# Half-block loads in 2 KB rows, turned by a permuted identity, with a new order for the opening

## The chip, the core and the metric

The kernel runs on one core of a Trainium2 chip. A core has a matrix engine (PE, with its weight loads, PEld, listed apart), a vector engine (DVE), a scalar engine (ACT), a general engine (POOL) and a queue engine (SP) that issues most DMAs. The metric is the device time of one execution in microseconds. The kernel before takes 397.38 us, the median of three runs (397.12 to 397.79).

## The reference

```python
def _attn_ref(x, f_logit, lower_bound):          # (4, 6144, 256), (4, 6144, 256), (256,)
    sig = 1.0 / (1.0 + np.exp(-f_logit))
    f = lower_bound[None, None, :] + (1.0 - lower_bound[None, None, :]) * sig
    i = 1.0 - f
    for t in range(S):
        h = f[:, t] * h + i[:, t] * x[:, t]
        y[:, t] = h

def _moe_ref(x, w1, w2, w_out):                  # x: (24576, 256), the y of above
    g = np.maximum(x @ w1, x @ w2)               # (24576, 1024)
    return g @ w_out                             # (24576, 256), float32
```

A gated recurrence runs over 6144 tokens of each of four sequences, 256 channels wide; a maxout layer with 1024 hidden units and an output projection follow, token by token.

## The kernel before

The 24576 tokens are cut into 48 blocks of 512. The recurrence wants channels on partitions and tokens along the row (scan, L142, runs along the row), while the inputs have tokens first, so every block must be turned.

The maxout is rewritten as max(h1, h2) = h1 + relu(h2 - h1). The hidden matmuls use wd, the scaled difference of w2 and w1; the h1 part goes straight to the output by a 256 x 256 matrix w13, the product of w1 and w_out. A block so has 16 hidden matmuls of 512 columns (L245), eight relus (L240) and 40 output matmuls of 256 columns (L268).

Blocks 4 to 47 come in pairs: a DMA from POOL casts them to bf16 in DRAM (cast, L167), a DMA transpose from SP brings them in turned (turn_dma, L176), and the loop at L565 goes over blocks and hidden units, PE's hidden matmuls of block j beside the output of block j - 1. That part is the same in both kernels.

Blocks 0 to 3 are the opening, and the change lies there. They are loaded as they lie, in f32, by SP (load, L96): blocks 0 to 2 in halves of 256 tokens (256 KB), block 3 whole. Partition p gets token q * 128 + p for row q of a tile, so a packet is one token's 1 KB. ACT forms u = sigmoid(-f) (gate_nat, L107), DVE v = u * x (drive_nat, L112), both bf16. PE turns each (turn_pe, L120) by four transposes of 128 x 128 against the bf16 identity ident_b into a bf16 PSUM tile; forget (L132) makes the decay from the turned u on ACT or DVE, and the scan takes the decay and the turned v.

At the same time the weights come in as twelve loads of 256 KB, four quarters k of each of w1, w2 and w_out, and are prepared: rounded (RW, RO), subtracted (D), scaled (SC), w1 turned (TW), copied out of PSUM (KW), multiplied into w13 (W13) and kept (KL).

The order of all this is written out by hand in two lists. LOADS (L445) is the order on SP. f0a is the first half of block 0's f, x0b the second half of its x, w13 the quarter 3 of w1. At most eight of SP's loads are in flight: the ninth waits for the landing of the first that holds its semaphore. PLAN (L449) is the order of the compute steps; each engine runs its own steps in this order and waits where an input is late. In a step's name G is gate, V drive, TU and TV the turns of u and v, F forget, S scan, H a hidden matmul group, R relu, P and L output matmuls, O the copy of an output tile; digits are block, half (a, b) and channel half or unit; the ending .a, .v or .p names ACT, DVE or POOL. warm3 is three matmuls on zeros that keep PE busy. CA starts the first cast and the first DMA transposes.

[...]

Of the kernel before, what the change touches and what calls it, by code (L numbers as in the profile page):

```python
# [8 lines left out]
FP32 = mybir.dt.float32  # L9
BF16 = mybir.dt.bfloat16  # L10
ALU = mybir.AluOpType
AF = mybir.ActivationFunctionType
P = 128
# [3 lines left out]
def kernel(  # L17
# [13 lines left out]
    nc = tc.nc  # L31
# [4 lines left out]
    KC = D // P  # L36
    FC = DFF // P
    TB = 512
    HB = TB // 2
    NQ = TB // P  # L40
# [8 lines left out]
    const = ctx.enter_context(tc.tile_pool(name="const", bufs=1))  # L49
# [14 lines left out]
    ps_d = ctx.enter_context(tc.tile_pool(name="ps_d", bufs=5, space=PS))  # L64
    ps_o = ctx.enter_context(tc.tile_pool(name="ps_o", bufs=3, space=PS))

    ident = const.tile([P, P], FP32)
    ident_b = const.tile([P, P], BF16)
    warm = const.tile([P, TB], BF16)
    held = const.tile([P, 1], FP32)  # L70
    om = const.tile([P, KC], FP32)
# [10 lines left out]
    w13 = wpool.tile([P, KC, D], BF16)  # L82


    ins, us, vs, uT, vT, ffs, ys = {}, {}, {}, {}, {}, {}, {}

    def alloc_in(j):
        fn = inpool.tile([P, NQ, D], FP32, name="fn")
        xn = inpool.tile([P, NQ, D], FP32, name="xn")
        ins[j] = (fn, xn)  # L90
        us[j] = natpool.tile([P, NQ, D], BF16, name="un")
        vs[j] = natpool.tile([P, NQ, D], BF16, name="vn")
        ffs[j] = nffpool.tile([P, KC, TB], BF16, name="nff")
        ys[j] = ypool.tile([P, KC, TB], BF16, name="y")

    def load(j, s, half=None):  # L96

        src = (f_logit, x)[s]
        q0, q1 = (0, NQ) if half is None else (2 * half, 2 * half + 2)
        nc.sync.dma_start(  # L100
            out=ins[j][s][:, q0:q1, :],
            in_=src[0, j * TB + q0 * P : j * TB + q1 * P, :].rearrange(
                "(q p) d -> p q d", p=P
            ),
        )

    def gate_nat(j, q0, q1):  # L107
        nc.scalar.activation(  # L108
# [10 lines left out]

    def turn_pe(j, s, x):  # L120

        dst = (uT, vT)[s][j, x] = ps_d.tile([P, KC, HB], BF16, name="dT")
        src = (us, vs)[s][j]
        for q in range(2):
            for h in range(KC):
                nc.tensor.transpose(  # L126
                    dst[:, h, q * P : (q + 1) * P],
                    src[:, 2 * x + q, h * P : (h + 1) * P],
                    ident_b[:],
                )  # L130

    def forget(o, i, h, on_act=False):  # L132
# [43 lines left out]
    def turn_dma(c):  # L176
        for s, name in enumerate(("fs", "xs")):
            t = ttpool.tile([P, KC, CB * TB], BF16, name=("fT", "xT")[s])
            turned[c, s] = t
            nc.sync.dma_start_transpose(out=t[:], in_=spare[c % NS, name][:])  # L180

    def cast_behind(c):

        if c + 1 < NCH:
            last = CB * TB - 1
            nc.gpsimd.tensor_copy(out=held[:], in_=turned[c, 0][:, KC - 1, last : last + 1])  # L186
            cast(c + 1)
# [5 lines left out]
    def gate(j):  # L193
        ffs[j] = midpool.tile([P, KC, TB], BF16, name="ff")
        ys[j] = ypool.tile([P, KC, TB], BF16, name="y")
        us[j] = midpool.tile([P, KC, TB], BF16, name="u")
        nc.scalar.activation(out=us[j][:], in_=part(j, 0), func=AF.Sigmoid, scale=-1.0)  # L197

    def drive(j):
        vs[j] = midpool.tile([P, KC, TB], BF16, name="v")  # L200
        nc.vector.tensor_tensor(out=vs[j][:], in0=us[j][:], in1=part(j, 1), op=ALU.mult)  # L201

    def forget_half(j, h, on_act=False):
        forget(ffs[j][:, h, :], us[j][:, h, :], h, on_act)

    def scan_half(j, h):
        scan(j, h, 0, TB, vs[j][:, h, :])
# [45 lines left out]
    def hidden(j, fc):  # L253
        hidden_whole(j, fc)
        relu(j, fc)
# [49 lines left out]
    def project(j, slot):  # L305
        i, half_ = divmod(slot, 2)
        n = FC + KC
        project_steps(j, i, half_ * n // 2, (half_ + 1) * n // 2)
# [17 lines left out]
    def store(j, g):  # L326
        copy_out(j, g)
        send_out(j, g)

    def store_row(j, g, r):  # L330
        osb = lastpool.tile([P, D], FP32, name="row")
        nc.vector.tensor_copy(out=osb[:], in_=pos[j, g, r][:, 0, :])  # L332
        r0 = j * TB + 2 * g * P
        nc.sync.dma_start(
            out=out[r0 : r0 + 2 * P, :].rearrange("(p r) d -> p r d", r=2)[:, r, :],
            in_=osb[:],
        )
# [93 lines left out]
    def keep_warm(n):  # L431
        for _ in range(n):
            nc.tensor.matmul(  # L433
                idle[:].rearrange("p r d -> p (r d)"),
                lhsT=warm[:, 0:P],
                rhs=warm[:],
                start=True,
                stop=True,
            )
# [3 lines left out]


    LOADS = """  # L445
    f0a x0a f0b w13 w23 x0b w12 w22 wo3 w10 w20 w11 wo2 w21 f1a x1a wo0 f1b x1b wo1
    f2a f2b x2a x2b f3 x3
    """
    PLAN = """  # L449
    G0a RW3.p keeps_T keeps V0a TU0a D31.p warm3 TV0a D30.p G0b F0a0.v warm4 TU0b  # L450
    D21.p F0a1.v S0a1 S0a0 V0b F0b1.a warm1 TW3 F0b0.a RW0.p warm5 TV0b RW2.v S0b1
    D01.p KW3.a TW2 SC31.a SC30.a KW2.a S0b0 RO3.a H06a H07a D20.v SC21.a warm3 H06b
    SC20.v H07b D00.v W133 RW1.v R07.a TW0 H04b H04a RO2.p H05a R06.a P071 SC00.v
    H05b P070 P061 D10.p TW1 SC01.a KW0.v R05.a R04.v H01a KW1.v H00a H00b H01b P040
    P050 P060 G1a P041 SC10.v V1a W132 R01.a D11.p TU1a RO0.p SC11.a P051 TV1a R00.a
    H02a F1a1.v F1a0.a RO1.p H03b S1a1 P011 G1b H02b S1a0 P010 H03a R02.a W130 V1b
    P001 R03.a TU1b H17a F1b1.v P000 TV1b H15a F1b0.a S1b1 S1b0 G2a H16a P031 P030
    P021 G2b W131 KL1.v TU2a F2a0.a P020 H17b H15b KL0.v H16b L01 L11 R17.a TU2b
    H10a H10b R16.a V2a R15.v F2a1.v H11b O01.a P161 H11a TV2a F2b0.a H12b P151 L10
    P171 V2b H12a R11.a F2b1.v R10.a S2a1 TV2b S2a0 G3b P150 R12.a S2b1 G3a L00 S2b0  # L460
    H13a V3b TU3b O00.a H13b P101 R13.a F3b1.v H14a P160 F3b0.v H14b P100 P170 H20
    H26 V3a TU3a P111 F3a1.v H21 R14.a H27 R20.a F3a0.v R26.a TV3a S3a1 P120 H24
    TV3b R21.a P121 P110 S3a0 H22 R27.a S3b1 P130 R24.a R22.a S3b0 H23 P131 R23.a
    H25 P140 O10.v P141 R25.a O11.v CA
    """

    engines = {"a": nc.scalar, "v": nc.vector, "p": nc.gpsimd}
# [1 line left out]
    def load_item(name):  # L469
        if name[:2] == "wo":  # L470
            wout_load(int(name[2]))
        elif name[0] == "w":
            w, src = ((w1n, moe_w1), (w2n, moe_w2))[int(name[1]) - 1]
            weight_load(int(name[2]), w, src)
        else:
            half = ("ab".index(name[2]),) if len(name) == 3 else ()
            load(int(name[1]), "fx".index(name[0]), *half)
# [8 lines left out]
    def issue(item):  # L486
# [10 lines left out]
        elif kind in ("G", "V") and len(arg) == 2:  # L497
            (gate_nat if kind == "G" else drive_nat)(arg[0], 2 * arg[1], 2 * arg[1] + 2)
        elif kind in ("TU", "TV"):
            turn_pe(arg[0], "UV".index(kind[1]), arg[1])  # L500
        elif kind == "F" and len(arg) == 3:
            j, x, h = arg
# [48 lines left out]
    with tc.manual_schedule():  # L551
        for j in range(NP):
            alloc_in(j)
        nc.scalar.dma_start(out=lbr[:], in_=lower_bound.rearrange("(h p) -> h p", p=P))
        for name in LOADS.split():
            load_item(name)
        nc.vector.memset(warm[:], 0.0)  # L557
        make_identity(nc, ident[:])
        nc.vector.tensor_copy(out=ident_b[:], in_=ident[:])
        keep_warm(7)  # L560
        for item in PLAN.split():
            issue(item)
        assert not outs

        for j in range(3, NBLK + 1):  # L565
            for fc in range(FC):
                if j < NBLK:
                    hidden(j, fc)
                project(j - 1, fc)
                if fc == 0 and j > 3:  # L570
                    store(j - 2, 1)
                if fc == 4 and j < NBLK:
                    store(j - 1, 0)
                if j == NBLK and fc in (3, 5, 7):
                    if fc == 3:
                        store(j - 1, 0)
                    else:
                        store_row(j - 1, 1, (fc - 5) // 2)
                if (j, fc) in gate_of:
                    b = gate_of[j, fc]  # L580
                    gate(b)
                    drive(b)
                    for h in range(KC):
                        forget_half(b, h)
                        scan_half(b, h)
                if (j, fc) in turn_of:
                    turn_dma(turn_of[j, fc])
                    cast_behind(turn_of[j, fc])
# [30 lines left out]
```

## Time and profile before

| what | value |
|---|---|
| median of three runs | 397.38 us |
| the profiled execution | 397.38 us |
| its span | 395.6 us |
| PE busy | 387.6 us (98%) |
| ACT busy | 273.3 us (69%) |
| DVE busy | 251.2 us (63%) |
| POOL busy | 39.2 us (10%) |
| granted PE clock | full in all slices but the last (0.97) |
| first half-block load of f issued, landed | 0.74, 3.6 us |
| second half of block 0's x issued, landed | 3.29, 8.71 us |
| first hidden matmul of the loop over blocks | 36.0 us |

The page gives for each engine the time it was busy, as a share of the span. Busy time of PE is the union of pipelined matmuls, so a matmul's own duration (219 ns for 128 columns, 272 for 256) is longer than the step from one to the next; the steps are read from the chain of work that ended last, which follows back from the last instruction what released each one. The list of waits says for which producer an engine sat idle. The DMA view counts packets and the time they took as a share of sixteen DMA engines.

### The profile page before, as it was taken

Reading aid. Unit: us, or ns where it says so; the run is one execution under the profiler, and the core shown is the slowest. Engines: PE = TensorE matmul, PEld = TensorE weight load, DVE = VectorE, ACT = ScalarE, POOL = GpSimd, SP = SyncE. Lnnn points to the kernel's source line nnn. Section 1 sums busy time; section 2 is a strip of 40 time slices with the busy share of each in tenths; the row PEclk is TensorE's granted clock in tenths of the full one; section 3 lists DMA queues with packets and bytes.
Section 4 is the critical chain, followed back from the end, with each engine's and each line's share of the span. In section 5 each row is a group of like instructions: output and inputs, shape, how many; then the busy total and the mean of one; then the engine's idle time right before and its main releaser. Section 6 shows DMA issues by size and latency. Waiting matters only on the chain.

```text
span 395.6 us, 7146 instructions
## 1 busy us (share of the span) xinstructions
PE 387.6 (98%) x2793; PEld 275.0 (70%) x2840; DVE 251.2 (63%) x366; ACT 273.3 (69%) x451; POOL 39.2 (10%) x83
## 2 busy tenths in 40 slices
PE   8999999999999999999999999999999999999996
PEld 3796777676667777767677777666677777676775
DVE  4896965756755775576567656755775576567622
ACT  4787676677667666766676677667766766676661
POOL 2511011011101101001011011011011010100000
PEclk9999999999999999999999999999999999999999
DMA  7989999999999999999999999999898898981122
GB/s 252 350 220 211 211 206 216 216 221 225 200 228 201 203 230 178 229 220 202 199 232 209 188 228 191 195 208 230 198 204 213 186 202 193 217 188 55 53 81 107
DMA packets 125078, 79.12 MB, mean 200 GB/s; under 512 B 94194, under 2 KB 101620, under 8 KB 125044
## 3 DMA queue, kind: packets, MB, share of 16 engines
q1 hardware_dynamic: 113072, 55.59, 59.8%
q0 software_dynamic: 11968, 23.07, 35.7%
q8 instruction: 22, 0.36, 0.4%
q14 instruction: 12, 0.10, 0.1%
q10 hardware_dynamic: 4, 0.00, 0.0%
HBM read 53.48 MB, written 48.23 MB: 257 GB/s over the span
## 4 chain that ended last, share of the span: by engine, by line
PE 95%; DMA 1%; DVE 1%; issue 1%; SPq 1%; DVEq 0%
PE psO L268 53%; PE dT L245 39%; PE dT L225 2%; DMA xn<-in_x_dram 1%; PE dT L126 1%; SPq L100 0%; PE psO L413 0%; DVE vn L113 0%; SPq L344 0%; DVE y L149 0%; DVE wd L388 0%; DVE wdf L380 0%; DVE row L332 0%; PE dT L396 0%; DVEq L113 0%
## 5 line engine op out<-in xcount | busy, mean ns | idle before, releaser
L240 ACT ACTIVATE rt<-dT 128x512 bf16<-128x512 f32 x382 | 222.9, 596 | 104.4 <-PE dT L245 101.2
L268 PE MATMUL psO<-wob,rt 128*128 128x256 bf16 x1536 | 231.0, 273 | 0.2
L268 PEld LDWEIGHTS <-rt 128*128 128x128 bf16 x1536 | 150.0, 98 | 94.7 <-issue 0.2
L245 PE MATMUL dT<-y,wd 128*128 128x512 bf16 x690 | 208.8, 379 | 2.2
L149 DVE TENSOR_TENSOR_SCAN y<-ff,y,v 128x512 bf16<-128x512 bf16 x82 | 105.2, 1283 | 2.9
L317 DVE COPY osb<-psO 128x512 f32<-128x512 f32 x93 | 62.6, 678 | 65.6 <-PE psO L268 65.6
L245 PEld LDWEIGHTS <-wd 128*128 128x128 bf16 x736 | 72.0, 98 | 8.8
L268 PE MATMUL psO<-w,y 128*128 128x256 bf16 x384 | 72.4, 273 | 0.0
L201 DVE TENSOR_TENSOR v<-u,xT 128x1024 bf16<-128x1024 bf16 x44 | 30.4, 691 | 62.7 <-ACT u L197 50.8
L197 ACT ACTIVATE u<-fT 128x1024 bf16<-128x1024 bf16 x44 | 46.1, 1049 | 3.1 <-DMA fT<-fs 3.1
L268 PEld LDWEIGHTS <-y 128*128 128x128 bf16 x384 | 37.6, 98 | 4.4
L186 POOL CAST held<-fT 128x1 f32<-128x1 bf16 x21 | 6.7, 319 | 278.9 <-DMA fT<-fs 278.9
L138 DVE TENSOR_SCALAR ff<-u,nom 128x512 bf16<-128x512 bf16 x88 | 29.7, 338 | 0.0
L170 POOL DMA_DIRECT2D fs<-in_f_logit_dram x22 | 12.3, 558 | 4.3 <-issue 4.3
L170 POOL DMA_DIRECT2D xs<-in_x_dram x22 | 12.1, 549 | 0.0
L149 DVE TENSOR_TENSOR_SCAN y<-nff,y,dT 128x256 bf16<-128x256 bf16 x14 | 9.6, 731 | 1.8 <-PE dT L126 1.5
L225 PE MATMUL dT<-y,wd 128*128 128x256 bf16 x64 | 10.1, 273 | 0.3 <-DVE wd L388 0.2
L433 PE MATMUL psO<-warm 128*128 128x512 bf16 x22 | 7.8, 492 | 1.2 <-DVE warm L557 1.2
L149 DVE TENSOR_TENSOR_SCAN y<-ff,v 128x512 bf16<-128x512 bf16 x6 | 7.4, 1225 | 0.2
L108 ACT ACTIVATE un<-fn 128x512 bf16<-128x512 f32 x8 | 5.0, 628 | 3.3 <-DMA fn<-in_f_logit_dram 3.0
L225 PEld LDWEIGHTS <-wd 128*128 128x128 bf16 x64 | 5.8, 98 | 1.4 <-issue 0.4
L113 DVE TENSOR_TENSOR vn<-un,xn 128x512 bf16<-128x512 bf16 x8 | 6.1, 767 | 1.0 <-DMA xn<-in_x_dram 1.0
(40 smaller groups left out, 52.2 us busy)
## 6 DMA issues: line engine op xcount, KB each, us to landing
out_dram<-osb SPq DMA_DIRECT2D x95, 256.0 KB, 3.4
fs<-in_f_logit_dram POOLq DMA_DIRECT2D x22, 512.0 KB, 6.8
xs<-in_x_dram POOLq DMA_DIRECT2D x22, 512.0 KB, 9.6
fn<-in_f_logit_dram SPq DMA_DIRECT2D x6, 256.0 KB, 6.0
xn<-in_x_dram SPq DMA_DIRECT2D x6, 256.0 KB, 5.7
w1n<-in_moe_w_dram SPq DMA_DIRECT2D x4, 256.0 KB, 5.9
w2n<-in_moe_w_dram SPq DMA_DIRECT2D x4, 256.0 KB, 6.0
won<-in_moe_w_out_dram SPq DMA_DIRECT2D x4, 256.0 KB, 6.0
```

What stands on the lines that cost most here:

```text
L138: nc.vector.tensor_scalar(out=o, in0=i, scalar1=nom[:, h : h + 1], scalar2=1.0, op0=ALU.mult, op1=ALU.add)
L149: nc.vector.tensor_tensor_scan(out=ys[j][:, h, t0:t1], data0=ffs[j][:, h, t0:t1], data1=v, initial=initial, op0=ALU.mult, op1=ALU.add,)
L170: nc.gpsimd.dma_start(out=spare[c % NS, name][:], in_=src[b, k * TB : (k + CB) * TB, :], max_dma_last_dim=4096,)
L186: nc.gpsimd.tensor_copy(out=held[:], in_=turned[c, 0][:, KC - 1, last : last + 1])
L197: nc.scalar.activation(out=us[j][:], in_=part(j, 0), func=AF.Sigmoid, scale=-1.0)
L201: nc.vector.tensor_tensor(out=vs[j][:], in0=us[j][:], in1=part(j, 1), op=ALU.mult)
L225: nc.tensor.matmul(dts[j, fc][:, tok], lhsT=wd[:, kc, unit(fc)], rhs=ys[j][:, kc, tok], start=(first and kc == 0), stop=(not first and kc ...
L240: nc.scalar.activation(out=rt[:], in_=dts[j, fc][:], func=AF.Relu)
L245: nc.tensor.matmul(dts[j, fc][:], lhsT=wd[:, kc, unit(fc)], rhs=ys[j][:, kc, :], start=(kc == 0), stop=(kc == KC - 1),)
L268: nc.tensor.matmul(ps, lhsT=lhsT, rhs=rhs, start=start, stop=stop, skip_group_check=True)
L317: nc.vector.tensor_copy(out=osbs[j, g][:], in_=pos[j, g, 0][:])
L433: nc.tensor.matmul(idle[:].rearrange("p r d -> p (r d)"), lhsT=warm[:, 0:P], rhs=warm[:], start=True, stop=True,)
```

## The change

Half-block loads take their tokens in another order. Within 256 tokens, token 32 i + 2 e + r goes to partition 8 e + i, row r, with e from 0 to 15. Two neighbouring tokens so lie together in a partition, a packet is 2 KB, and the sixteen groups e read side by side through DRAM. Block 3, loaded whole, keeps the old layout.

The turn has to put the tokens back. For blocks 0 to 2 the moving operand is ident_s, the identity with its columns permuted, made by one more DVE copy; each matmul's result goes to every second column of the PSUM tile (r, r + 2, ...). A transpose in bf16 is replaced by a plain matmul with f32 output, for block 3 too, there with ident_b and packed columns. [...]

The two lists are new. In LOADS the first six stay; then come w11 w21 f1a x1a ahead of the other weights, and x3 ahead of f3. In PLAN the second quarter of weights prepared is 1 and not 2, block 1's gate, turns and drive come earlier, many scales, roundings and relus change engine, and CA stands earlier. The warm-up matmuls are 20 instead of 23 (the seven ahead of PLAN included); all other PE work is the same in number.

```diff
     def load(j, s, half=None):
         src = (f_logit, x)[s]
-        q0, q1 = (0, NQ) if half is None else (2 * half, 2 * half + 2)
-        nc.sync.dma_start(
-            out=ins[j][s][:, q0:q1, :],
-            in_=src[0, j * TB + q0 * P : j * TB + q1 * P, :].rearrange(
-                "(q p) d -> p q d", p=P
-            ),
-        )
+        if half is None:
+            o = ins[j][s][:]
+            i = src[0, j * TB : (j + 1) * TB, :].rearrange("(q p) d -> p q d", p=P)
+        else:
+            t0 = j * TB + half * HB
+            o = ins[j][s][:, 2 * half : 2 * half + 2, :]
+            i = src[0, t0 : t0 + HB, :].rearrange("(i e r) d -> e i r d", e=16, r=2)
+        nc.sync.dma_start(out=o, in_=i)
...
     def turn_pe(j, s, x):
-        dst = (uT, vT)[s][j, x] = ps_d.tile([P, KC, HB], BF16, name="dT")
+        dst = (uT, vT)[s][j, x] = ps_d.tile([P, KC, HB], FP32, name="dT")
         src = (us, vs)[s][j]
-        for q in range(2):
+        for r in range(2):
             for h in range(KC):
-                nc.tensor.transpose(
-                    dst[:, h, q * P : (q + 1) * P],
-                    src[:, 2 * x + q, h * P : (h + 1) * P],
-                    ident_b[:],
+                nc.tensor.matmul(
+                    dst[:, h, r:HB:2] if j < 3 else dst[:, h, r * P : (r + 1) * P],
+                    lhsT=src[:, 2 * x + r, h * P : (h + 1) * P],
+                    rhs=(ident_s if j < 3 else ident_b)[:],
+                    start=(r == 0 and h == 0),
+                    stop=(r == 1 and h == KC - 1),
+                    skip_group_check=True,
                 )
...
     LOADS = """
-    f0a x0a f0b w13 w23 x0b w12 w22 wo3 w10 w20 w11 wo2 w21 f1a x1a wo0 f1b x1b wo1
-    f2a f2b x2a x2b f3 x3
+    f0a x0a f0b w13 w23 x0b w11 w21 f1a x1a wo3 w12 w22 wo1 f1b wo2 x1b w10 w20 f2a
+    wo0 f2b x2a x2b x3 f3
     """
     PLAN = """
-    G0a RW3.p keeps_T keeps V0a TU0a D31.p warm3 TV0a D30.p G0b F0a0.v warm4 TU0b
-    D21.p F0a1.v S0a1 S0a0 V0b F0b1.a warm1 TW3 F0b0.a RW0.p warm5 TV0b RW2.v S0b1
-    D01.p KW3.a TW2 SC31.a SC30.a KW2.a S0b0 RO3.a H06a H07a D20.v SC21.a warm3 H06b
-    SC20.v H07b D00.v W133 RW1.v R07.a TW0 H04b H04a RO2.p H05a R06.a P071 SC00.v
-    H05b P070 P061 D10.p TW1 SC01.a KW0.v R05.a R04.v H01a KW1.v H00a H00b H01b P040
...
+    keeps_T RW3.p G0a keeps TU0a V0a D30.p F0a0.a F0a1.v D31.p warm3 TV0a G0b D10.p
+    S0a1 warm3 TU0b D11.p RO3.p warm1 TW3 F0b1.a S0a0 RW2.p F0b0.a V0b D21.p warm5
+    TV0b KW3.a SC30.v RW1.a S0b0 warm1 TW1 SC31.a H07a S0b1 G1a KW1.v H06a H07b
+    SC10.a SC11.v TU1a V1a H06b H03b H03a F1a0.v H02b R07.a W133 R06.a D20.v P070
+    SC21.v P061 RO1.p P071 P060 R03.a TW2 H02a F1a1.a KW2.v TV1a SC20.a H05a S1a0
+    R02.a H05b W131 RO2.v G1b P020 H04a H04b TU1b V1b P031 RW0.p R05.a F1b0.a P021
+    S1a1 W132 R04.a TV1b D00.p P051 D01.p P030 TW0 H15a RO0.p F1b1.a P041 S1b0 S1b1
...
+    H10a F2b1.a F2b0.a H13a V2b P150 TV2b P120 P170 L10 H10b S2a1 G3a O00.v R13.a
+    P151 TU3a G3b P160 F3a1.a P111 S2a0 P131 P001 R10.a S2b0 CA TU3b L01 F3a0.a S2b1
...
         nc.vector.tensor_copy(out=ident_b[:], in_=ident[:])
+        nc.vector.tensor_copy(
+            out=ident_s[:].rearrange("p (i e) -> p i e", e=16),
+            in_=ident[:].rearrange("p (e i) -> p i e", e=16),
+        )
         keep_warm(7)
```

More of the change, by code (lines that the diff above doesn't have):

```diff
@@ L68 @@
     ident_b = const.tile([P, P], BF16)
+    ident_s = const.tile([P, P], BF16)
     warm = const.tile([P, TB], BF16)
@@ L453 @@
-    SC20.v H07b D00.v W133 RW1.v R07.a TW0 H04b H04a RO2.p H05a R06.a P071 SC00.v
-    H05b P070 P061 D10.p TW1 SC01.a KW0.v R05.a R04.v H01a KW1.v H00a H00b H01b P040
[L455 to L464, printed above, removed]
+    keeps_T RW3.p G0a keeps TU0a V0a D30.p F0a0.a F0a1.v D31.p warm3 TV0a G0b D10.p
@@ new lines @@
+    P050 P040 SC00.a SC01.a H12a KW0.v H16a H15b H16b H12b G2a H00a R15.v H01b H00b
+    R16.v H01a H17b R12.a H17a H11b H14a R00.a H11a G2b R01.v W130 P011 TU2a H14b
+    P010 V2a KL1.v KL0.v R17.a R11.a F2a1.v TU2b R14.a TV2a P000 F2a0.a H13b L00
+    H10a F2b1.a F2b0.a H13a V2b P150 TV2b P120 P170 L10 H10b S2a1 G3a O00.v R13.a
+    P151 TU3a G3b P160 F3a1.a P111 S2a0 P131 P001 R10.a S2b0 CA TU3b L01 F3a0.a S2b1
+    F3b1.v V3a P110 P130 F3b0.a H23 V3b R23.a P161 P171 H24 O01.v P140 R24.a H22
@@ L465 @@
+    TV3a R22.a S3a0 H21 H25 S3a1 R21.a TV3b H20 P100 P141 H26 R25.a P101 O10.a H27
+    S3b0 S3b1 R27.v P121 L11 R20.a O11.v R26.a
     """
```

## The prediction

> **What bounds the kernel now.** I read the page first: how much of the span the matrix engine fills, and which chain ends last.
>
> ```profile
> span 395.6 us, 7146 instructions
> PE 387.6 (98%) x2793; PEld 275.0 (70%) x2840; DVE 251.2 (63%) x366; ACT 273.3 (69%) x451; POOL 39.2 (10%) x83
> ...
> PE 95%; DMA 1%; DVE 1%; issue 1%; SPq 1%; DVEq 0%
> ```
>
> PE is the bound, and the change touches the first 36 us alone. So the second reading was PE's list of waits from 13.5 us on, which has one row (0.2 us for wd, at 13.45), and the third the chain in order of time from 0 to 14 us:
>
> ```profile
> 3.29 5.42 DMA xn<-in_x_dram
> ...
> 8.80 1.21 DVE vn L113
> ...
> 11.22 0.72 DVE y L149
> 11.94 0.72 DVE wdf L380
> ...
> 12.68 0.73 DVE wd L388
> ...
> 13.45 0.61 PE dT L225 x4
> ```
>
> The reader is to see one string: the fourth half-block load (x0b) lands at 8.71, the drive product V0b follows, then the scans, then one scale of wd, and from 13.45 PE is never again without work. The end is therefore "when PE becomes gapless" plus "all PE work not yet done by then". The change can act through these two terms only. From the same chain, later, comes what work costs on PE when nothing else limits it:
>
> ```profile
> 17.56 0.22 PE dT L126 x4
> ...
> 18.23 0.44 PE dT L225 x4
> ```
>
> A turn (four matmuls of 128 columns) is 0.22 us, 55 ns each; a matmul of 256 columns is 109 ns. Next the timeline of DVE and POOL around the start:
>
> ```profile
> 8.05 1.41 POOL L380 TENSOR_TENSOR wdf<-w2n,w1n 128x256 f32<-128x256 f32 x2 [0.58 <-DMA w2n<-in_moe_w_dram]
> 8.80 1.20 DVE L113 TENSOR_TENSOR vn<-un,xn 128x512 bf16<-128x512 bf16 x1 [0.96 <-DMA xn<-in_x_dram]
> 12.68 0.72 DVE L388 TENSOR_SCALAR wd<-wdf,om 128x256 bf16<-128x256 f32 x1
> 13.99 0.34 DVE L388 TENSOR_SCALAR wd<-wdf,om 128x256 bf16<-128x256 f32 x1
> ```
>
> The same drive product took 0.68 at 4.73 with POOL idle and 1.20 here beside POOL's subtraction; the same scale took 0.34 or 0.72. Last the DMA view of three stretches (10 to 18, 2 to 8.7, 386.5 to 391 us):
>
> ```profile
> DMA packets 2911, 2.81 MB, mean 351 GB/s; under 512 B 172, under 2 KB 2911, under 8 KB 2911
> q1 hardware_dynamic: 2911, 2.81, 109.3%
> ```
> ```profile
> DMA packets 2132, 2.06 MB, mean 308 GB/s; under 512 B 120, under 2 KB 2132, under 8 KB 2132
> ```
> ```profile
> DMA packets 164, 0.27 MB, mean 61 GB/s; under 512 B 31, under 2 KB 31, under 8 KB 164
> q1 hardware_dynamic: 164, 0.27, 16.4%
> ```
>
> **The change part by part.** The sum is made on the profiled execution: 397.38 us, a span of 395.6 and 1.78 around it, which is also the median of the three runs.
>
> *Loads.* In the first stretch 2739 packets of 1 KB took 1.093 x 16 x 8 = 139.9 us of engine time, 51 ns each (47 net of the overlap over 100%). In the last, 133 packets of 2 KB (stores) took 0.164 x 16 x 4.5 = 11.8 us, 89 ns each. A half-block is 16 packets of 1 KB an engine now, 16 x 47 = 0.75 us, and becomes 8 of 2 KB, 8 x 89 = 0.71, or 0.65 if these overlap as much. I take 0.065 saved; four half-blocks up to x0b give 0.26. Besides, the stretch 2 to 8.7 ran at 308 GB/s and not 351, a loss of 6.7 x (1 - 308/351) = 0.82; no row shows if a side-by-side sweep cures it. Bounds: nothing saved and one half-block's time lost (+0.75), or all of both saved (-1.1). I take a third of the loss, 0.27, since the sweep touches four of six loads and a late engine may have other causes. So x0b lands at 8.71 - 0.53 = 8.2. SP issues the same 26 loads, eight in flight; the later ones land sooner still (8 x 0.065 = 0.5), and PE waits for none of them now.
>
> [...]
>
> *The order from x0b to gapless.* New DVE order: V0b, scale SC30, two scans, copy KW1, scale SC11, which frees matmul group H03. From rows: 0.09 (landing to V0b) + 1.21 + 0.72 + 1.38 (the two scans at 10.56) + 0.04 for steps = 3.44 until the scans end; then 0.41 (w1T copy at 14.25) + 0.72 + 0.05: gapless at x0b + 4.62. I take the slow 0.72 of both scales because POOL runs D10, D11, RO3 and RW2 in a row there, 0.72 + 0.72 + 0.62 + 0.61; with 0.34 for each it would be 0.76 less, though then PE's own H07b, TU1a and H06b (0.92 if the turn is slow) set it at x0b + 3.98. Now it is 13.45 - 8.71 = 4.74. But less is done by then. Before 13.45 PE now finishes four turns of block 0, three of w1, eight matmuls of 256 columns and the W133 group (0.44); then it will have the same without W133, three turns (TW3, TW1, TU1a) in place of TW3, TW2, TW0. Equal ends so need gapless at 13.45 - 0.44 = 13.01. It comes at 8.2 + 4.62 = 12.82: -0.19 us. Warm-up matmuls fall from 23 to 20; they fill idle time.
>
> Waits that the new order adds on ACT: G1a now stands ahead of scale SC10 and needs f1a, ninth in the list. Each load behind x0b takes 0.75 or 0.69, so f1a lands at x0b + 0.75 + 0.75 + 0.69 = 10.4, G1a ends by 11.05 (0.63) and SC10 by 11.57 (0.51), before SC11 starts at 12.05: hidden by 0.5, and a later f1a costs what exceeds that. w10 and w20 move back behind x1b, to about 17.5; D00 and D01 on POOL (0.72 each) end near 19, SC00 and SC01 near 20, H00 is reached near 21.5: hidden by some 1.5.
>
> *The turns.* Blocks 0 to 2 turn by plain matmul with f32 output on every second column of PSUM. The trace has no stepped output. Lower end: 55 ns, as the packed 128-column turn. Upper end: 109 ns, the 256-column f32 matmul, whose 256 words of PSUM are the span that 128 stepped columns cover. The new form shares only the column count with the first row, and output type and span with the second; I take 109. Four turns of block 0 lie in waits for DMA or behind SC30, and TU1a in the wait for SC11; seven turns (TV1a, TU1b, TV1b, four of block 2) lie where PE is gapless: 7 x 4 x 54 ns = +1.51 us. Block 3 keeps packed columns: 0.
>
> [...]
>
> *At nothing, with what hides it.* The ident_s copy (0.23, the row of ident_b) lies in DVE's 3.02 us of idle time before 4.59. Readers of f32 in PSUM: the DVE relu reads 512 columns in 0.67, so 256 take 0.34, the bf16 forget's own 0.34; ACT 0.47 against half of 0.60. The scan takes 0.69 for 256 columns, twice what reading f32 asks; were it a tenth slower, two scans on the path cost 0.14. Moved roundings, scales and relus change engine but not number: PE waited for none after 13.45, and ACT and DVE are 69% and 63% busy; if that cover fails, a late relu costs its 0.6. The first cast of the DMA-turned chunk (CA) moves in the list, yet on POOL it still follows the last RO and on SP its turns still follow the 26 loads, so nothing passes it. The last two scans (1.38) get 2.6 us of PE work behind TV3b: hidden. From 36 us the program is the same.
>
> Sum: -0.19 + 1.51 = +1.32, so 398.7 us.
>
> **The rivals.**
> 1. *Faster: the early loads close up.* Were the startup loss and more gone and the stepped output free, x0b could land at 7.2: gapless 11.82, -1.19 us, 396.2. For it: 308 against 351 GB/s, and landings of f0b 1.8 us behind x0a where the rate asks 0.75. Against: the weights in between keep their rows. With free turns it is faster by over 0.2% (0.8 us, about what a measurement of this kernel can tell from no change) once x0b lands by 7.6; with slow turns it would need 6.1.
> 2. *The turns stay at 55 ns* and loads gain as I take: -0.19, 397.2. For it: bf16 and f32 outputs both go at one column per 0.43 ns here. Against: none of these is stepped.
> 3. *The last load gates ACT.* Now x3 is last (it landed at 26.73), and f3 will be; G3a stands on ACT ahead of R13, G3b and F3a, and PE wants TU3a near 28. With the half-blocks' 0.8 us saved f3 lands near 26: no wait. Past 27 each us is one on PE; at 28 with slow turns, some +2, 399.4.
> 4. *2 KB rows change nothing* (x0b at 8.71): +0.32 from the order alone, with the turns 399.2.
>
> **How the numbers follow.** Slow turns with about these loads (forecast and 4 together) 0.56, nearly all slower, some 0.06 within the bound where the loads gain most. Rival 2: 0.19, nearly all same. Rival 1: 0.19. Rival 3: 0.06. So faster 0.19, same 0.26, slower 0.55. The likeliest case's own range: x0b between 7.6 and 9.0 gives 398.1 to 399.5. The range over all runs from between rivals 1 and 2, 396.5, to 399.5.
>
> **What will show it.** A turn's four matmuls in the chain (0.43 or 0.22 us a turn); x0b's landing (V0b's start near 8.3) and packet time of 2 KB loads; gapless PE from about 12.8; no wait of G3a for f3; span equal to 395.6 + 1.3. Wrong if turns step at 55 ns, if x0b lands before 7.6, or if PE shows new waits after 13 us.

## The result, and the profile after

The changed kernel takes 402.56 us, the median of four runs (401.36 to 403.83), against 397.27 us for the kernel before, run on the same chip: a ratio of 1.0131, 95% interval 1.0094 to 1.0169. In another comparison it was 1.0132 (1.0117 to 1.0147). It is slower, as forecast, but by about 5.3 us where 1.3 were forecast, and above the range. The profiled execution took 403.32 us, 5.9 more than the profiled execution before.

The page of the kernel after, span, matrix engine and shares of the chain that ended last:

```profile
span 401.5 us, 7141 instructions
...
PE 391.9 (98%) x2791; PEld 277.4 (69%) x2837; DVE 251.4 (63%) x363; ACT 273.3 (68%) x453; POOL 38.8 (10%) x85
...
PE 78%; DMA 16%; DVE 2%; SPq 2%; issue 1%; POOL 0%; POOLq 0%; DVEq 0%
```

PE has 95% of the chain before and 78% after; DMA has 16% where it had 1%. The busy share of PE, 98% in both, says nothing of this. The chain in order of time, from 0 to 42 us, shows which transfers (start, us, what):

```profile
3.89 0.55 SPq L107
...
5.12 7.41 DMA w2n<-in_moe_w_dram
...
12.54 7.72 DMA won<-in_moe_w_out_dram
...
20.28 9.36 DMA xn<-in_x_dram
29.64 0.05 issue
29.69 0.12 POOL held L542
29.82 5.02 DMA fs<-in_f_logit_dram
...
34.85 6.90 DMA fT<-fs
```

It is one string of loads, each of 7 to 9 us, from 5 to 30 us: the 8th, the 16th and the 24th of SP's list. The 16th and the 24th were each issued within 0.02 us of the landing of the one eight places ahead (12.54 behind 12.53, 20.28 behind 20.27). Before, the loads left the chain at 8.71. Here the chain goes on through the second half of block 2's x (20.28, landed 29.64) and then into the first cast of the loop's input. The DMA view of 10 to 18 us gives the reason. Before, this stretch moved 2.81 MB at 351 GB/s; after:

```profile
DMA packets 1900, 2.21 MB, mean 277 GB/s; under 512 B 132, under 2 KB 1507, under 8 KB 1900
...
q1 hardware_dynamic: 1900, 2.21, 109.5%
```

The sixteen DMA engines are as full as before (109.5% and 109.3%) and move a fifth less. In the trace's packet records, from 10 to 26 us, a 2 KB packet of these loads took 123 to 144 ns (medians of stretches of 2 us; 14 to 16 us, with 11 such packets, is left out), where the stores of the kernel before gave 89. A 1 KB packet that runs beside them took 65 to 86 ns from 16 us on, where it took 46 to 51 before.

The vector engine's timeline from the landing of x0b (10.39 us, 1.68 later than before) on:

```profile
10.48 1.09 DVE L115 TENSOR_TENSOR vn<-un,xn 128x512 bf16<-128x512 bf16 x1 [0.97 <-DMA xn<-in_x_dram]
11.50 0.34 DVE L393 TENSOR_SCALAR wd<-wdf,om 128x256 bf16<-128x256 f32 x1
12.34 1.39 DVE L154 TENSOR_TENSOR_SCAN y<-nff,y,dT 128x256 bf16<-128x256 bf16 x2 [0.50 <-ACT wd L395]
13.64 0.40 DVE L360 COPY w1T<-dT 128x512 bf16<-128x512 bf16 x1
14.04 0.35 DVE L393 TENSOR_SCALAR wd<-wdf,om 128x256 bf16<-128x256 f32 x1
```

and PE's list of waits from 13 to 75 us (us in total, times, longest; dT are the PSUM tiles of turns and hidden sums, psO those of the output):

```profile
PE dT L128 <- DVE vn L115: 0.6, 1, 0.6
PE dT L230 <- DVE y L154: 0.4, 1, 0.4
PE psO L273 <- ACT rt L245: 0.4, 2, 0.2
PE psO L418 <- POOL wob L360: 0.2, 1, 0.2
PE dT L230 <- ACT wd L395: 0.2, 1, 0.2
```

Before, one row stood there:

```profile
PE dT L225 <- DVE wd L388: 0.2, 1, 0.2
```

Three rows of after can be followed to a late load. The drive of block 1's second half (PE waits 0.6 us, until 22.00) had waited for its x; the rounding on POOL (0.2 us, until 15.84) for its quarter of w_out; the scale on ACT (0.2 us, until 18.36) for a subtraction on DVE that had waited 1.08 us for its quarter of w2. The scan (0.4 us, until 13.77) is the last of block 0, behind x0b. The instructions of the turn's line on PE, minimum, median and maximum duration in ns, show the second cost:

```profile
L128 PE MATMUL dT<-ident_s,vn x20: 272/314/314, 11.6 to 31.8; 128*128 128x128 bf16 x20
L128 PE MATMUL dT<-ident_s,un x16: 272/314/314, 14.1 to 29.1; 128*128 128x128 bf16 x16
L128 PE MATMUL dT<-ident_b,un x8: 219/219/219, 33.2 to 34.5; 128*128 128x128 bf16 x8
```

A stepped matmul takes 314 ns, a packed one (block 3) 219. From start to start the trace has 109 ns in blocks 0 to 2 and 55 to 56 in block 3, though both write f32.

To put the parts together: take the PE work (output and hidden matmuls) that is still to do at some time before, and ask when the kernel after has as much left. It is some 1.7 us late at 13 us, as x0b's landing was; 3.4 at 16; 4.3 at 20; 5.5 at 28; 5.3 from 36 to 52; 6.0 from 54 on. The listed waits up to 36 us (0.6 + 0.4 + 0.2 + 0.2 = 1.4) and the stepped turns (seven or eight at 0.22, some 1.6) make 4.7 with the 1.7. The other 0.6 of the 5.3 is not traced to a row; the last step up, after 52 us, is told below.

### The profile page after: what moved, and what is told of

Same layout as the page of the kernel before. It is cut to its first block, busy times and chain, and to the rows that moved or that the text cites. A ratio compares the mean times of both kernels' runs of the same rounds, so it can differ in the third digit from the quotient of the medians.

```text
span 401.5 us, 7141 instructions
## 1 busy us (share of the span) xinstructions
PE 391.9 (98%) x2791; PEld 277.4 (69%) x2837; DVE 251.4 (63%) x363; ACT 273.3 (68%) x453; POOL 38.8 (10%) x85
## 4 chain that ended last, share of the span: by engine, by line
PE 78%; DMA 16%; DVE 2%; SPq 2%; issue 1%; POOL 0%; POOLq 0%; DVEq 0%
PE psO L273 45%; PE dT L250 34%; DMA fs<-in_f_logit_dram 5%; DMA fT<-fs 4%; DMA xn<-in_x_dram 2%; DMA won<-in_moe_w_out_dram 2%; DMA w2n<-in_moe_w_dram 2%; DMA xT<-xs 1%; DVE y L154 1%; SPq L185 1%; SPq L107 1%; SPq L349 0%; DVE v L206 0%; DVE osb L322 0%; DVE ff L143 0%
## 5 line engine op out<-in xcount | busy, mean ns | idle before, releaser
L250 PEld LDWEIGHTS <-wd 128*128 128x128 bf16 x736 | 71.9, 98 | 8.5
L191 POOL CAST held<-fT 128x1 f32<-128x1 bf16 x21 | 5.3, 254 | 279.6 <-DMA fT<-fs 279.6
L139 ACT ACTIVATE nff<-dT,nom 128x256 bf16<-128x256 f32 x12 | 5.4, 474 | 4.8 <-PE dT L128 3.7
```

The lines of the kernel that those rows point to most:

```text
L250: nc.tensor.matmul(dts[j, fc][:], lhsT=wd[:, kc, unit(fc)], rhs=ys[j][:, kc, :], start=(kc == 0), stop=(kc == KC - 1),)
```

## The experiments

### Each part alone

**The two lists alone.** Both LOADS and PLAN of the kernel after in the kernel before, with loads and turns as before.

> The kernel before with the two new lists alone; loads and turns as before. Theory A (the loss lies in loads and turns, the lists are nearly neutral): x0b lands near 8.7 as before, PE gapless near 13.3, +0.3 us by the prediction's sum for the order, so 397.2 to 398.0. Theory B (the new order itself makes late waits, for example G3a behind f3 or SC waits): a PE gap of over 0.3 us behind 14 us and +1 us or more.

Measured: 397.53 against 397.48 us, ratio 1.0005 (0.9996 to 1.0013). The new lists change nothing that can be told.

**The swept loads alone.** The load of the kernel after in the kernel before:

```diff
+            i = src[0, t0 : t0 + HB, :].rearrange("(i e r) d -> e i r d", e=16, r=2)
```

> [...] The turns stay as they were, so tokens of blocks 0 to 2 are in another order and the output of those blocks is not the reference's. Theory A (the sweep makes packets slow): 2 KB packets of the loads take 120 to 140 ns as in the changed kernel, x0b lands near 10.4, x2b near 27.5 and not 23.7, and the time is +3 to +4.5 us. Theory C (the packets are slow there only because of the new order of loads): packets near 90 ns, x0b at 8.5, 397.0.

Measured: 401.38 against 397.48, ratio 1.0114 (1.0098 to 1.0131). Most of the loss is here. x0b landed at 9.94, 2 KB packets took 123 to 145 ns, and PE was 1.1 us late at 12 to 16 us and 3.7 to 3.9 from 24 on. The second loss can be seen in its chain from 13 to 30 us, where a load of w_out ends last:

```profile
14.28 10.06 DMA won<-in_moe_w_out_dram
...
24.39 0.62 POOL wob L356
...
25.06 0.81 PE psO L269 x6
```

A load of weights, whose own rows nobody changed, took 10 us from issue to landing (13.22 to 19.24, 6.0 us, in the kernel before), and PE waited 1.5 us for it at 25 us. So the sweep costs the loads between its own as well.

**The stepped turns alone.** The turn of the kernel after (with ident_b) in the kernel before, with its loads:

```diff
-                nc.tensor.transpose(
-                    dst[:, h, q * P : (q + 1) * P],
...
+                nc.tensor.matmul(
+                    dst[:, h, r:HB:2] if j < 3 else dst[:, h, r * P : (r + 1) * P],
...
```

> The kernel before with only the new turn: plain matmuls with f32 output on every second column of PSUM for blocks 0 to 2, with the unpermuted identity. Loads as before, so tokens of blocks 0 to 2 are in another order and the output of those blocks is not the reference's. Theory A (109 ns a step instead of 55, and PE pays for it where it is gapless): eight turns of blocks 1 and 2 times 0.216 us, +1.5 to +1.9 us. Theory E (turns are partly hidden in waits): +0.9 us or less.

Measured: 399.33 against 397.48, ratio 1.0053 (1.0039 to 1.0066), that is +1.85 us. In its chain from 10 to 34 us a turn now is

```profile
18.05 0.44 PE dT L126 x4
...
18.70 0.44 PE dT L126 x4
...
21.10 0.44 PE dT L126 x4
...
30.71 0.22 PE dT L126 x4
```

0.44 us for the stepped ones and 0.22 for block 3. Eight stand in the gapless part (18 to 30 us), 8 x 0.22 = 1.7; the other 0.1 is within the uncertainty (the interval of the ratio is 1.6 to 2.6 us), and the last turn of block 0, ahead of a scan, may be in it. A matmul of 128 columns of f32 on every second word so takes 109 ns here, and a packed one 55. No other step was run.

**2 KB rows without the sweep.** The loads as in the sweep, but partition p takes tokens 2p and 2p + 1:

```diff
+            i = src[0, t0 : t0 + HB, :].rearrange("(p r) d -> p r d", r=2)
```

> [...] Turns as before, so tokens of blocks 0 to 2 are in another order and the output of those blocks is not the reference's. Theory A (it is the sweep, not the row size): 2 KB packets near 90 ns, x0b near 8.5, -0.3 to 0 us. Theory D (a 2 KB row as such is slow to load): packets of 120 to 140 ns, x0b near 10.4, +3 us and more as in the swept kernel.

Measured: 396.66 against 397.48, ratio 0.9987 (0.9976 to 0.9997); 2 KB packets took 84 to 89 ns, x0b landed at 8.17. One landing is weak evidence by itself: with the old rows x0b landed at 8.32, 8.71 and 9.17 in three profiles that issue the same first six loads (the lists alone, the kernel before, the turns alone). The rate says more. From 16 to 20 us the DMA view shows, first for the kernel before, then for these rows, then for the sweep:

```profile
DMA packets 1422, 1.39 MB, mean 347 GB/s; under 512 B 81, under 2 KB 1421, under 8 KB 1421
```
```profile
DMA packets 968, 1.51 MB, mean 376 GB/s; under 512 B 89, under 2 KB 391, under 8 KB 967
...
q1 hardware_dynamic: 967, 1.49, 104.2%
```
```profile
DMA packets 700, 0.99 MB, mean 248 GB/s; under 512 B 63, under 2 KB 368, under 8 KB 700
...
q1 hardware_dynamic: 700, 0.99, 108.5%
```

Rows of 2 KB do gain: 376 GB/s, where the kernel before had 347 with 1 KB rows. With the sweep the same 2 KB rows moved at 248, a third less.

**The changed kernel with these rows.** The sweep replaced by the blocked rows in the kernel after, turned with ident_b:

> [...] New lists and stepped turns stay; nothing is left out. Theory A (the three parts add up: lists 0, stepped turns +1.9, blocked loads -0.8 against before): 398.0 to 399.0. Theory F (the parts multiply: the new lists need the sweep, or the stepped turn costs more there): over 399.5.

Measured: 398.45 against 397.49, ratio 1.002 (1.0011 to 1.0029). Of the 5.3 us, 4.3 are gone. What is left, +0.96, is near the sum of the parts: +0.05 (lists), +1.85 (turns), -0.82 (rows) = +1.08. So without the sweep the parts add up. Its vector engine's timeline is the one that the prediction had worked out:

```profile
8.55 1.24 DVE L115 TENSOR_TENSOR vn<-un,xn 128x512 bf16<-128x512 bf16 x1 [1.18 <-DMA xn<-in_x_dram]
9.71 0.34 DVE L393 TENSOR_SCALAR wd<-wdf,om 128x256 bf16<-128x256 f32 x1
10.56 1.39 DVE L154 TENSOR_TENSOR_SCAN y<-nff,y,dT 128x256 bf16<-128x256 bf16 x2 [0.50 <-ACT wd L395]
11.86 0.40 DVE L360 COPY w1T<-dT 128x512 bf16<-128x512 bf16 x1
12.17 0.73 DVE L393 TENSOR_SCALAR wd<-wdf,om 128x256 bf16<-128x256 f32 x1
```

x0b landed at 8.46, and the last scale, which frees H03b, ends at 12.90, x0b + 4.44; the prediction had 4.57 to that point (its 4.62 less the step of 0.05).

### Do the turns cost on top of the late loads?

The changed kernel with packed turns, the sweep kept:

```diff
-                    dst[:, h, r:HB:2] if j < 3 else dst[:, h, r * P : (r + 1) * P],
+                    dst[:, h, r * P : (r + 1) * P],
```

> The changed kernel with its sweep and its lists, but each turn's results on packed columns: the tokens of blocks 0 to 2 stay in another order, so the output of those blocks is not the reference's. Theory A (the parts add up): 1.9 us less than the changed kernel, 400.4 to 401.2. Theory O (turns hide in the waits that the late loads make): within 1 us of the changed kernel's 402.6.

Measured: 402.61 us (401.49 to 405.37), ratio 1.0149 (1.0108 to 1.019): no gain by the medians. The profiled execution, though, has a span of 399.7, 1.8 less than the changed kernel's. A second comparison has both kernels side by side.

> The changed kernel once more, for an interval taken beside that of the next kernel. Both theories: 401.4 to 404 us, 1.010 to 1.017 of before.

> The changed kernel with packed columns in its turns (the sweep's loads stay, so the tokens of blocks 0 to 2 come out in another order and the output is not the reference's), again, beside the changed kernel. Theory A (the turns' 1.85 us add to the lateness of the loads): 1.5 to 2 us less than the changed kernel of this call. Theory O (the turns hide behind PE's waits for the late loads): within 0.5 us of it.

Measured: 403.13 us (402.39 to 404.12) for the changed kernel and 401.78 us (399.45 to 404.69) with packed turns, ratios 1.0132 (1.0117 to 1.0147) and 1.0114 (1.0078 to 1.015). The medians differ by 1.35, the intervals overlap, and so do the runs. The profiled executions differ by 2.4 us of span (402.3 and 399.9). This stays open. The sum of the parts alone, +0.05 + 3.90 + 1.85 = +5.8 against the +5.3 and +5.4 measured, suggests that some half microsecond of the turns is hidden, but the interval of the +5.3 alone is 3.7 to 6.7 us; the medians of the first comparison allow that all of it is. Runs with the sweep and packed turns spread most: 5.2 us over six, where 21 runs of the kernel before lie within 1.5 and within 2.3 us in two comparisons.

### What makes the sweep slow

All kernels of this part are the kernel before with half-block loads that differ only in the source pattern, in rows of 2 KB but for one of 1 KB. They read other tokens for blocks 0 to 2, so their output there is not the reference's. Their times are single executions, and the packet times carry the verdict. The first thought was the addresses: with the sweep, sixteen groups of rows lie 2 KB apart, and within a group each row lies 32 KB behind the one before. Were all groups read at once, sixteen places close together would be read at a time. That they are, each by a DMA engine of its own as the expectations have it, is the author's assumption; no trace here tells which engine moved a row.

```diff
+            i = src[0, t0 : t0 + 8 * 34, :].rearrange("(i w) d -> i w d", w=34)
+            i = i[:, 0:32, :].rearrange("i (e r) d -> e i r d", r=2)
...
+            i = src[0, t0 : t0 + 16 * 258, :].rearrange("(e w) d -> e w d", w=258)
+            i = i[:, 0:256, :].rearrange("e (i w) d -> e i w d", w=32)[:, :, 0:2, :]
```

The first keeps the groups 2 KB apart and makes the step 34 KB, the second puts the groups 258 KB apart and keeps the step of 32.

> [...] Theory G (the engines hinder each other because they read within the same 32 KB at a time): packets stay at 120 to 140 ns. Theory H (an engine's own step of 32 KB, a power of two, is what is slow): near 90 ns.

> [...] Theory G (closeness of the engines): near 90 ns, x0b near 8.2. Theory H (the step of 32 KB): 120 to 140 ns, x0b near 10.

Both stayed slow: 399.09 us and packets of 104 to 146 ns, 401.23 us and 113 to 142 ns, beside 397.49 for the kernel before. Neither the nearness of the groups nor the even step alone is the cause. Next, even steps of 4 and of 16 KB from partition to partition, and rows of 1 KB that jump by 16 KB:

```diff
+            i = src[0, t0 : t0 + 128 * 4, :].rearrange("(p w) d -> p w d", w=4)
+            i = i[:, 0:2, :]
...
+            i = src[0, t0 : t0 + 128 * 32, :].rearrange("(p w) d -> p w d", w=32)
+            i = i[:, 0:32:16, :]
```

> [...] Other tokens are read for blocks 0 to 2, so the output of those blocks is not the reference's. Theory K (any jump between 2 KB rows is slow): packets of 120 to 140 ns. Theory L (only long jumps are slow, the 4 KB of the weights' rows are not): near 90 ns.

> [...] Theory K: 120 to 140 ns. Theory L with a limit between 4 and 16 KB: 120 to 140 ns; with a limit above 16 KB: near 90 ns.

> [...] Theory M (the jump is slow whatever the row): packets of the f and x loads take well over 60 ns and x0b lands behind 9.5. Theory N (only 2 KB rows suffer): near 47 to 51 ns, x0b at 8.2 to 8.8.

All three had packets as fast as those of the blocked rows: 84 to 89, 84 to 91, and 46 to 51 ns for the 1 KB rows. Their times were 397.89, 397.39 and 398.31 us, beside 397.62 for the kernel before; x0b landed at 9.27, 8.74 and 9.67, so it can land late with fast packets too. What the three patterns with long packets have in common, and the others do not, is the form: the 128 rows are written as 16 groups of 8. Two patterns cross form and addresses:

```diff
+            t0 = (2 * j + half) * 16 * 18
+            i = src[0, t0 : t0 + 16 * 18, :].rearrange("(e w) d -> e w d", w=18)
+            i = i[:, 0:16, :].rearrange("e (i r) d -> e i r d", r=2)
...
+            i = src[0, t0 : t0 + 128 * 32, :].rearrange("(p w) d -> p w d", w=32)
+            i = i[:, 0:2, :]
```

> The kernel before with half-block loads of 2 KB rows whose source pattern is written as 16 groups of 8 rows: groups 18 KB apart, rows 2 KB apart within a group. The addresses are nearly those of the blocked pattern (one run of memory with a gap of 2 KB after every eighth row), the form of the pattern is that of the sweep. It loads other tokens than the reference wants, so its output is not the reference's. Theory P (the form of the pattern, three levels against two, is what makes the packets slow): 2 KB packets of 120 to 145 ns, x0b lands past 9.5, a span of 397 to 400 us. Theory A (the addresses that are read at one time make them slow): 84 to 95 ns, x0b near 8.2 to 9, a span near 395 to 396 us.

> The kernel before with half-block loads of 2 KB rows, partition p's row 32 KB behind that of p-1: a pattern of two levels (128 rows in one even step). It loads other tokens than the reference wants, so its output is not the reference's. The pattern with groups 258 KB apart and rows 32 KB apart within a group had packets of 113 to 142 ns. Theory P (form of the pattern): 84 to 95 ns, a span near 395 to 396.5 us. Theory A (rows a large step apart are slow to read): 110 to 145 ns, a span of 398 to 400 us.

The form tells them apart, and the addresses do not. Sixteen groups with near-blocked addresses: 400.43 us, 2 KB packets of 124 to 140 ns from 14 us on; rows an even 32 KB apart: 397.31 us, 85 to 89 ns (the kernel before: 397.71). From 16 to 20 us, the DMA view of the first and then of the second:

```profile
DMA packets 671, 0.96 MB, mean 240 GB/s; under 512 B 62, under 2 KB 341, under 8 KB 671
...
q1 hardware_dynamic: 671, 0.96, 108.3%
```
```profile
DMA packets 967, 1.50 MB, mean 375 GB/s; under 512 B 89, under 2 KB 396, under 8 KB 966
...
q1 hardware_dynamic: 966, 1.48, 103.9%
```

Is it any split in two levels, or the sixteen groups?

```diff
+            i = src[0, t0 : t0 + 32 * 10, :].rearrange("(e w) d -> e w d", w=10)
+            i = i[:, 0:8, :].rearrange("e (i r) d -> e i r d", r=2)
...
+            i = src[0, t0 : t0 + 64 * 6, :].rearrange("(e w) d -> e w d", w=6)
+            i = i[:, 0:4, :].rearrange("e (i r) d -> e i r d", r=2)
```

> As the kernel with 16 groups of 8 rows of 2 KB and a gap of 2 KB between groups, but with 32 groups of 4 rows: again three levels, near-blocked addresses, and an output that is not the reference's. Theory T (any pattern whose rows are split in two levels is slow): 2 KB packets of 120 to 145 ns, SP busy 0.58 us with one load, a span of 397 to 400 us. Theory N (it takes an outermost level of 16, one group per DMA engine): 84 to 95 ns, a span of 395 to 396.5 us.

> The same with 64 groups of 2 rows. Theory T: 120 to 145 ns and a span of 397 to 400 us; Theory N: 84 to 95 ns and a span of 395 to 396.5 us. Its output is not the reference's.

Thirty-two groups of 4 took 397.42 us, sixty-four of 2 took 398.32 (before: 397.12). Both had packets of 86 to 89 ns from 14 to 22 us, and from 16 to 20 us the first shows

```profile
DMA packets 993, 1.50 MB, mean 376 GB/s; under 512 B 88, under 2 KB 443, under 8 KB 992
...
q1 hardware_dynamic: 992, 1.49, 105.1%
```

So of the forms tried, slow packets come with the sixteen groups of 8 alone. The form is not enough by itself, though. The ranges above leave out the start: from 2 to 4 us the median of the 2 KB packets was 84 ns in all four patterns of sixteen groups too, while the packets took 78 to 88% of the sixteen engines' time and not the 101 to 112% of the later stretches; in the near-blocked one it stayed at 84 to 85 until 8 us. Whether it is fuller engines that make these packets slow, or the other loads in flight, was not tested.

One thing the sweep and the patterns of 16, 32 and 64 near-blocked groups share: SP spent longer on the issue, 0.66 to 0.70 us for the first half-block load where an even step of 2 KB rows had 0.40. The first load in the queue's timeline, of the 32 groups, then of the even 32 KB step:

```profile
0.74 0.66 SPq L107 DMA_DIRECT2D fn<-in_f_logit_dram  x1
```
```profile
0.74 0.40 SPq L107 DMA_DIRECT2D fn<-in_f_logit_dram  x1
```

In the kernel after it is 0.69, in the kernel before 0.47, and x0b is issued at 3.89 instead of 3.29. The three kernels with such long issues and fast packets (32 groups, 64 groups, 1 KB rows that jump) issued x0b at 3.87 to 3.92 and landed it at 9.13, 9.68 and 9.67, that is 0.4 to 1.0 us later than the kernel before. So 0.4 to 1.0 of the 1.68 us comes without slow packets, and some 0.7 to 1.3 with them; these are single profiles.

Why sixteen groups of 8 are slow is not shown: no run here tells which engine moved which rows, and the cause stays open.

### A version that is faster than both

2 KB rows should pay until x0b has landed, and stepped turns should cost nothing where PE waits anyway. Both point to block 0. So block 0 alone gets blocked rows and stepped turns, all else stays as before:

```diff
+        if j == 0:
+            o = ins[j][s][:, 2 * half : 2 * half + 2, :]
+            i = src[0, half * HB : (half + 1) * HB, :].rearrange("(p r) d -> p r d", r=2)
+            nc.sync.dma_start(out=o, in_=i)
+            return
...
+        if j == 0:
+            dst = (uT, vT)[s][j, x] = ps_d.tile([P, KC, HB], FP32, name="dT")
...
+                        dst[:, h, r:HB:2],
```

> The kernel before, but block 0 alone loaded in 2 KB rows (tokens 2p, 2p + 1 to partition p) and turned by stepped matmuls; blocks 1 to 3, the lists and all else as before; nothing is left out. Theory A (the only loads that bound the start are the four of block 0, and its turns lie in waits but for the last): x0b 0.5 us sooner, the last turn 0.2 us longer, so -0.3 us, 397.0 to 397.3. Theory I (the gain of the blocked loads comes from the later blocks): 0 to +0.3 us.

Measured: 397.05 against 397.49, ratio 0.9988 (0.9977 to 0.9999): about 0.4 us, just outside its uncertainty. The reason is not shown. In its profile x0b landed at 8.70, as in the kernel before (8.71), and not the expected half microsecond sooner; what was shorter there is the drive behind it:

```profile
8.79 0.69 DVE L118 TENSOR_TENSOR vn<-un,xn 128x512 bf16<-128x512 bf16 x1 [1.22 <-DMA xn<-in_x_dram]
```

It took 0.69 us where the kernel before needed 1.20, both beside POOL's subtractions, and this time POOL paid, with 1.93 us for its two where it took 1.41 before. A gain that rests on which of the two engines gives way need not be the rows'.

## Why the prediction was right or wrong

**The turns: right.** The upper end, 109 ns, was the right choice, and the reason given, that the stepped output spans 256 words, fits: block 3 writes f32 packed and stays at 55, so the output type is not it. A step of two is the only one that ran, so the span is not told from a fixed price for each word that stands apart. +1.51 was forecast for seven turns; alone they cost +1.85, with one more of them in the gapless part in the old order (8 x 0.22 = 1.7). The +1.51 was thus of the right size, while rival 2 fell.

**The loads: wrong, and this is the step that failed.** The prediction wrote "So x0b lands at 8.71 - 0.53 = 8.2" and let a half-block lose 0.75 us at worst. It landed at 10.39, +1.68. The price of a 2 KB packet by itself was right: 89 ns was taken, 84 to 89 measured with blocked rows. That x0b landed at 8.17 there, where 8.2 was forecast, is in part luck: it landed at 8.46 and 8.70 in the two other profiles with blocked rows, and the 0.27 for a cured startup rested on no row. What was missing is that the price of a packet was taken from its size alone, from stores of another pattern, and the sweep's pattern was costed as a possible cure for the startup loss, with no end for the case that it slows packets. A packet of 2 KB in 16 groups took 123 to 144 ns from 10 us on; at 140, and with the prediction's estimate of eight to an engine, that is 1.1 us a half-block instead of 0.71, and neighbours of 1 KB went from 47 to some 75 ns. The bound of +0.75 was one half-block wide, where the effect goes with every load in flight. The issue on SP, 0.55 to 0.69 us a half-block instead of 0.45 to 0.47, was not costed at all, and kernels with such issues and fast packets landed x0b 0.4 to 1.0 us late.

**"PE waits for none of them now": wrong for the same reason.** The prediction let the later loads land sooner and priced their lateness only in rival 3. With the rate down from 351 to 277 GB/s, block 1's f and x and the weights came after their slots, and PE waited 1.4 us for a drive, a scan, a rounding and a scale between 13 and 36 us. The prediction's own check, "if PE shows new waits after 13 us", caught it.

**The order: right in effect.** +0.32 by the order at an unchanged x0b, -0.19 with the loads' gain: measured +0.05 (interval about -0.2 to +0.5), with x0b at 8.32 in its profile. The chain V0b, scale, two scans, copy, scale ran as worked out: 4.44 of 4.57 us with blocked rows. The first scale took 0.34 and not 0.72, and a wait of 0.50 took up that gain. The view puts it down to ACT's scale, but the scan reads what PE's turn of V0b writes, and in that profile the turn's last matmul ended at 10.46, 0.10 before the scan began, where ACT's scale had ended at 10.27. So most likely the turn set the scan's start. The sum does not name it; behind a scale of 0.72 it would have been hidden.

**Rival 1** (loads close up, x0b by 7.6) had the sign of the loads wrong as the forecast did. **Rival 3** had the landing too early and the price too high: f3 was last and landed at 32.35, where 28 was the worst considered, and ACT stood idle 0.50 us for it, but PE's list has no wait there. By then PE was itself some 5.4 us late. **Rival 4** (rows change nothing) is refuted in the rate, 376 against 347 GB/s with blocked rows, and in their time, 0.82 us less; that they land x0b sooner is less sure.

**"From 36 us the program is the same": true, but not its start.** The prediction held that the first cast passes nothing. It stands behind a copy that reads the second half of block 2's x; that landed at 29.64 instead of 23.7, so the first DMA-turned chunk came at 41.76 instead of 35.24, and the second behind it at 57.07 instead of 50.88. The gate of the second waited for it, in the timeline of ACT:

```profile
57.18 1.06 ACT L202 ACTIVATE u<-fT 128x1024 bf16<-128x1024 bf16 x1 [1.95 <-DMA fT<-fs]
```

and PE, which then waited 0.4 us for two relus at 58.8 and 59.3, went from 5.3 to 6.0 us of lateness. That is a matter of this one execution: in the second profile of the changed kernel the same gate waited 1.3 us, and PE's list has no wait behind it. So a late load can cost PE something 20 us after the opening, but need not.

## What to carry to other kernels

Price a DMA by its pattern and not by its packet size alone (2 KB packets took 84 to 91 ns in even steps here and 109 to 146 in 16 groups of 8 from 14 us on): a row for the same bytes in another form is no row for this one, and the first look at such a change is the packet time and the GB/s in a stretch where the engines are full of these loads; at the start of the kernel, from 2 to 4 us, the swept rows showed 84 ns like the blocked ones. Loads in flight beside slow packets were slow too (1 KB packets went from 46 to 51 ns up to 65 to 86), so put the bound on all loads in flight, not on the one that is waited for. A layout that costs PE a stepped output (109 ns a matmul for 55, +1.85 us alone) is worth having here only for the work that lies in PE's waits, as in block 0.

## What the runs showed that was not expected

- 2 KB packets took 84 to 91 ns in patterns of one even step (2, 4, 16 or 32 KB) and 84 to 89 in 32 or 64 groups. In all four patterns of 16 groups of 8 rows, whatever their addresses, they took 109 to 146 ns from 14 us on, though 84 from 2 to 4 us; 1 KB packets beside them went from 46 to 51 ns up to 65 to 86 in the changed kernel.
- SP needed 0.40 us to issue the first half-block load in one even step of 2 KB rows, 0.47 in the old rows, and 0.66 to 0.70 in a pattern split in groups or in rows that jump.
- A matmul of 128 columns on every second f32 word of PSUM took as long here, from start to start, as one of 256 packed columns, 109 ns.
